# Keeping w_out's float32 blocks in DRAM and making its Winograd sums from them

## The chip, the cores and the metric

The kernel runs on one core of one Trainium2 chip. The metric is the device time of one execution in microseconds; times before and after are medians of several runs, and one further execution is recorded by the hardware profiler. The engines in the profile are PE (TensorE: matmuls) with PEld (its weight loads), DVE (VectorE), ACT (ScalarE), POOL (GpSimd) and SP (SyncE, which here only issues DMAs). An engine executes its own instructions strictly in the order written, and waits on semaphores for what other engines or DMAs deliver.

## The reference

The program is linear attention with random features, followed by a gated feed-forward layer. Cut to what matters:

```python
def phi(x):                                   # x: q or k, scaled by D ** -0.25
    h = np.einsum('bhsd,md->bhsm', x, omega) - np.sum(x * x, -1, keepdims=True) / 2
    return np.exp(h - h.max(-1, keepdims=True)) / np.sqrt(m)
q_p, k_p = phi(q_s), phi(k_s)                 # batch 8, heads 8, 576 tokens, D 64, m 128
kv = np.einsum('bhsm,bhsd->bhmd', k_p, v)
z = np.sum(k_p, axis=2)
num = np.einsum('bhsm,bhmd->bhsd', q_p, kv)
den = np.einsum('bhsm,bhm->bhs', q_p, z)[..., None] + 1e-06
x = (num / den) -> (4608 tokens, 512)
h = x @ w_in                                  # 512 x 2048, float64 in memory
g = h * np.tanh(softplus(h))
out = (g @ w_out).astype(np.float32)          # 2048 x 512, float64 in memory
```

## The kernel before

The 4608 tokens are worked in 18 chunks of 256. Matrix products are done in float16: each float32 operand is split into a high half (a cast, `cast`, L71) and a low half (the rest, `rest`, L80), and three of the four half products are summed. PE alternates between two streams: pieces of `ff_in(c)` (x times w_in, L804) and pieces of `ff_out(c-1)` (g times w_out, L1133). Between them stand the feature products of k and q (L416, with ek, eq, mxk, mxq as their results on VectorE) and the attention products (pkv L536, pn L587). Chunk 0 is computed in plain float32 (`ff_in(0)`, `ff_out0`) while the weights are still being scaled and split.

**Chunks 15, 16 and 17** use Strassen-Winograd: both products are done as seven products of half-sized blocks instead of eight (`ff_in7`, `ff_out7`). For this, sums of w_in's blocks (s1 to s4) and of w_out's blocks (t1 to t4) are needed. They are made in advance, during the chunks from 2 on, sent to DRAM as high and low float16 halves, and fetched again late in the kernel (`ask_sum`, `fetch_t`).

**How the weights come in.** A weight block is 1 MB of float64 words; there are eight blocks of w_in and eight of w_out. `w_task` (L200) loads a block, and turns it into float32 with integer operations on ScalarE (L211) and VectorE (L213, L217). The largest absolute value of each block is taken (L224 for w_in, L226 for w_out). When all eight are there, a power of two is made of the largest (`w_scale`: am_w L239, then, for w_out, over PE: row_w L136 and every_w L148), and `w_split` (L249) scales each block and splits it into its two halves. The splits write over the float32 blocks: after `w_split` the slots hold only the halves.

**How the sums are made.** `t_make(j)`, j from 0 to 3, makes the four sums for one pair of w_out's blocks, `s_make(gr, hb)` those of one pair of w_in's. Both call `sums_make` (L832). The operands are read as halves, so a difference of two blocks is two differences and an addition. Each result is cast (ScalarE) and its rest taken (VectorE) into a tile `xs`, and sent to DRAM by SP.

**What sets the order.** The program is written as generators on an agenda. A slot is one call of `step()` (L1230), 16 of them a chunk; `yield n` puts a generator to sleep for n slots. The makes are started by the loop at L1321 to L1323: first the four `t_make`, then the four `s_make`, 19 slots apart, from 40 slots after the end of chunk 0:

```python
makes = [(t_make, (j,)) for j in range(4)] + [(s_make, (i // 2, i % 2)) for i in range(4)]
for i, (fn, arg) in enumerate(makes):
    at(slot[0] + 40 + 19 * i, lambda fn=fn, arg=arg: start(fn(*arg)))
```

The framework's planner then places each engine's instructions by this order and by its own estimate of when operands are ready. Tiles with one tag share a fixed number of buffers: `ht` has five (`HB`), used by the hidden layer's tiles `h` and by the makes; `xs` has two; the PSUM tag `a` has four, shared by the feature and attention products.

Of the kernel before, what the change touches and what calls it, by code (L numbers as in the profile page):

```python
# [9 lines left out]
F16 = mybir.dt.float16  # L10
F32 = mybir.dt.float32
# [4 lines left out]
ALU = mybir.AluOpType  # L16
# [14 lines left out]
def tile_kernel(  # L31
# [10 lines left out]
    nc = tc.nc  # L42
    P = 128
    NT, D, H, _ = qT.shape
    B, HP, _, _, S = kT.shape
    M = omT.shape[1]
    DM, DF = w_in.shape
# [14 lines left out]
    sb = ctx.enter_context(tc.tile_pool(name="sb", bufs=2))  # L62
# [4 lines left out]
    dram = ctx.enter_context(tc.tile_pool(name="dram", bufs=1, space=bass.MemoryType.DRAM))  # L67

    act, dve, pool = nc.scalar, nc.vector, nc.gpsimd

    def cast(eng, out, in_, scale=1.0):  # L71

        if eng is act:
            act.activation(out, in_, AF.Copy, scale=scale)  # L74
        elif isinstance(scale, float) and scale == 1.0:
            eng.tensor_copy(out, in_)  # L76
        else:
            eng.tensor_scalar_mul(out, in_, scale)

    def rest(eng, out, in_, hi, scale=1.0):  # L80

        if isinstance(scale, float) and scale == 1.0:
            eng.tensor_tensor(out=out, in0=in_, in1=hi, op=ALU.subtract)  # L83
        else:
            eng.scalar_tensor_tensor(  # L85
                out=out, in0=in_, scalar=scale, in1=hi, op0=ALU.mult, op1=ALU.subtract
            )
# [85 lines left out]
    NB = 8  # L173
    BW = KT * DF // NB
# [3 lines left out]
    def flat32(slot):  # L178
        return slot.rearrange("p a b -> p (a b)").bitcast(F32)

    def fetch_w(n, i, dma):
        src = w_src[n](i)


        at = ({0: 0, 1: 1, 2: 2, 3: 3}, {7: 0, 6: 1, 3: 0})[n].get(i)
        if at is not None:
            raw = wo_t[:, 2 * at:2 * at + 2].rearrange("p a b c -> p (a b c)").bitcast(I64)
        else:
            raw = sb.tile([P, BW], I64, tag="g", name=f"raw{i}", bufs=GB)
        dma.dma_start(out=raw.rearrange("p (a b) -> p a b", b=src.shape[2]), in_=src)  # L190
        return raw

    @contextmanager
    def behind(nth, first=0):
        with ExitStack() as st:
            for ins in anchors.get(nth, ())[first:]:
                st.enter_context(tc.issue_after(ins))
            yield

    def w_task(i, name):  # L200

        n = 0 if name == "wi" else 1
        raw = loaded.pop(f"w{n}_{i}", None) or fetch_w(n, i, w_dma)
        yield W_LOAD
        word = raw.bitcast(I32).rearrange("p (n two) -> p n two", two=2)
        low, high = word[:, :, 0], word[:, :, 1]
        dst = flat32(slots[w_at(n, i)])
        di = dst.bitcast(I32)
        with behind(AP[i] if n == 0 else None):
            m = high.bitcast(F32)  # L210
            act.activation(m, m, AF.Prelu, scale=2.0 ** -112, alpha=-(2.0 ** 32))  # L211
        with behind((AS, AO)[n][i], 1):
            dve.tensor_single_scalar(out=di, in_=low, scalar=29, op=ALU.logical_shift_right)  # L213
        yield W_GAP
        did("w", n, i)
        with behind((AN, AO)[n][i], 1):
            dve.scalar_tensor_tensor(  # L217
                out=di, in0=high, scalar=3, in1=di, op0=ALU.logical_shift_left, op1=ALU.bitwise_or
            )
        if n == 0:  # L220
            yield WSUM[i]
            rough = sb.tile([P, BW], F16, tag="xs", name=f"rough{i}", bufs=2)
            with behind(AP[i]):
                act.activation(rough, dst, AF.Abs, accum_out=wmax[n][:, i:i + 1])  # L224
            return
        dve.tensor_reduce(  # L226
            out=wmax[n][:, i:i + 1], in_=dst, axis=AX.X, op=ALU.max, apply_absolute_value=True
        )

    def w_at(n, i):  # L230

        return i + 1 if n == 0 else NB + i
# [37 lines left out]
    def did(*key):  # L270
        done[key] = done.get(key, 0) + 1

    def must(n, *key):
        assert done.get(key, 0) >= n, key
# [24 lines left out]
    for i in range(2):  # L299
        t = const.tile([P, 2, 10, D1], F16, name=f"vb{i}")  # L300
# [526 lines left out]
    sums = {}  # L827

    def block(sl, a, row):
        return sl[:, a, row * BW // 2:(row + 1) * BW // 2]  # L830

    def sums_make(key, blocks, first, shape):  # L832
        n = BW // 2
        must(1, "s", 0, NB - 1)
        must(1, "s", 1, 0)
        t = sb.tile([P, 2, n], F32, tag="ht", name=f"s{key[0]}_{key[1]}", bufs=HB)
        s, u = (t[:, i].rearrange("p (a b) -> p a b", a=shape) for i in range(2))
        b11, b12, b21, b22 = blocks

        def tt(out, in0, in1, op=ALU.subtract):  # L840
            dve.tensor_tensor(out=out, in0=in0, in1=in1, op=op)

        def send(op, src):
            o = sb.tile([P, 2, n], F16, tag="xs", name=f"{op}_{key[0]}_{key[1]}", bufs=2)
            cast(act, o[:, 0], src)
            yield 1
            rest(dve, o[:, 1], src, o[:, 0])
            sums[key[0], key[1], op] = dram.tile([P, 2, n], F16, name=f"d{op}_{key[0]}_{key[1]}")
            nc.sync.dma_start(out=sums[key[0], key[1], op], in_=o)
            yield 1  # L850

        ops = ("s1", "s2", "s4", "s3") if first is ALU.add else ("t1", "t2", "t4", "t3")
        tt(s, b22(0) if first is ALU.add else b12(0), b21(0) if first is ALU.add else b11(0), first)
        yield 1
        tt(u, b22(1) if first is ALU.add else b12(1), b21(1) if first is ALU.add else b11(1), first)
        yield 1
        tt(s, s, u, ALU.add)
        yield from send(ops[0], t[:, 0])
        if first is ALU.add:
            tt(s, s, b11(0))  # L860
            yield 1
            tt(s, s, b11(1))
        else:
            tt(s, b22(0), s)
            yield 1
            tt(s, s, b22(1), ALU.add)
        yield from send(ops[1], t[:, 0])
        last = b12 if first is ALU.add else b21
        tt(u, last(0), s)
        yield 1  # L870
        tt(u, u, last(1), ALU.add)
        yield from send(ops[2], t[:, 1])
        pair = (b11, b21) if first is ALU.add else (b22, b12)
        tt(s, pair[0](0), pair[1](0))
        yield 1
        tt(u, pair[0](1), pair[1](1))
        yield 1
        tt(s, s, u, ALU.add)
        yield from send(ops[3], t[:, 0])
        did("sums" if first is ALU.add else "tsums")  # L880

    def s_make(gr, hb):
        sl1, sl2 = slots[4 * gr + hb], slots[4 * gr + 2 + hb]
        blocks = [
            lambda a, sl=sl, row=row: block(sl, a, row).rearrange("p (a b) -> p a b", a=2)
            for sl in (sl1, sl2) for row in range(2)
        ]
        return sums_make((gr, hb), blocks, ALU.add, 2)

    def t_make(j):  # L890
        blocks = [
            lambda a, f=f, m=m: wo_block(j, a, f, m) for f in range(2) for m in range(2)
        ]
        return sums_make(("w", j), blocks, ALU.subtract, 2)

    def wo_block(j, a, half, m):

        sl = slots[NB + 1 + 4 * half + j]
        return sl[:, a].rearrange("p (f m) -> p f m", f=2)[:, :, m * DM // 2:(m + 1) * DM // 2]
# [270 lines left out]
    GB, HB, QB = 4, 5, 1  # L1170
# [76 lines left out]
    for t in range(NT):  # L1247
        last = (t * P + P - 1) // S
# [21 lines left out]
    s_w = [None, None]  # L1270
# [8 lines left out]
    for what in PREL.split():  # L1279
        i = int(what[1:] or 0)  # L1280
# [12 lines left out]
    for i in range(NB):  # L1293
        start(w_task(i, "wi"), WIS[i])
    for i in reversed(range(1, NB)):
        start(w_task(i, "wo"), WOS[i])
# [9 lines left out]
    next(fi, None)  # L1306
    fi, fo = ff_in(1), ff_out0()
    start(w_task(0, "wo"))
    at(slot[0] + W_LOAD + W_GAP + 2, scale_w, 1)
    for j in range(8):  # L1310
# [4 lines left out]
    for j in range(8):  # L1315
# [3 lines left out]
        step()  # L1319
    next(fo, None)  # L1320
# [3 lines that stand above are left out]
# [62 lines left out]
```

## Time and profile before

| | us |
|---|---|
| median of 3 runs | 932.29 (931.63, 932.29, 934.01) |
| profiled execution | 936.42 |
| its span, first to last instruction | 934.6 |
| mean granted clock of TensorE | 0.998 of full speed |

In the profile a row of a group gives the line, the engine, the operation, output<-inputs by the program's names, shapes, the count, then the busy time in us, the mean duration of one in ns, and the engine's idle time just before them with what ended it. A row of the timeline gives the start in us from the span's start, the length in us, the engine, and in brackets the idle time before it with what released it. A timeline row can merge several instructions of one kind (x12 is twelve of them). A row of the waits gives who waited for whom, the total in us, the number of times, and the longest. A row of windows gives a stretch and the busy us of each engine in it.

### The profile page before, as it was taken

To read this page: it belongs to the slowest core of one execution; us is meant where nothing else is said; L and a number is where in the kernel's file an instruction comes from. 1 tells how busy PE (TensorE), PEld (TensorE's weight loads), DVE (VectorE), ACT (ScalarE), POOL (GpSimd) and SP (SyncE) were. 2 spreads that over 40 slices of the span, in tenths; PEclk is the share of its full clock that TensorE was granted. 3 is DMA by queue.
4 is the path that set the end of the run, shared out by engine and by line. 5 is a ranking of instruction groups with operands and counts; after the bars stand their busy time and mean duration, and the time that the engine had idled before them with its cause. 6 is when DMAs were issued, how large, how long until landed. Compare 5 with 4: busy or idle time off the path is not lost. (4 is left out here: it accounts for less than half of the span.)

```text
span 934.6 us, 21079 instructions
## 1 busy us (share of the span) xinstructions
PE 919.6 (98%) x8795; PEld 686.1 (73%) x8795; DVE 701.7 (75%) x1196; ACT 666.3 (71%) x889; POOL 216.0 (23%) x133
## 2 busy tenths in 40 slices
PE   9899999999999999899999999999999999999998
PEld 6688766677777777677777777777777777679997
DVE  4899786987769588787687757878688756668774
ACT  6988778776876967778777777788786866345442
POOL 0000123432432133222223134231241232200000
PEclk9999999999999999999999999999999999999999
DMA  9897135424532356223443254513432146972521
GB/s 308 272 280 227 50 60 120 83 86 80 111 86 84 74 112 144 65 78 89 103 116 86 77 115 104 137 49 103 106 70 91 35 116 140 237 192 92 165 63 46
DMA packets 153055, 108.69 MB, mean 116 GB/s; under 512 B 112832, under 2 KB 125248, under 8 KB 152960
## 3 DMA queue, kind: packets, MB, share of 16 engines
q1 hardware_dynamic: 152640, 106.75, 44.1%
q8 instruction: 69, 1.13, 0.5%
q10 hardware_dynamic: 320, 0.59, 0.2%
q14 instruction: 26, 0.21, 0.1%
HBM read 63.14 MB, written 17.83 MB: 87 GB/s over the span
## 5 line engine op out<-in xcount | busy, mean ns | idle before, releaser
L804 PE MATMUL ph<-xT,w 128*128 128x256 f16 (+1 forms) x2816 | 342.4, 278 | 0.9 <-ACT xT L738 0.9
L1133 PE MATMUL po<-wo,g 128*128 128x512 f16 x1344 | 310.2, 381 | 0.0
L804 PEld LDWEIGHTS <-w 128*128 128x128 f16 x2688 | 260.9, 98 | 46.6 <-issue 1.4
L1133 PEld LDWEIGHTS <-g 128*128 128x128 f16 x1344 | 127.5, 98 | 133.7 <-issue 1.6
L83 POOL TENSOR_TENSOR sq<-fq,sq 64x1024 f16<-64x1024 f32 x31 | 71.2, 2296 | 258.5 <-ACT sq L74 178.3
L991 ACT ACTIVATE h<-ph,us 128x512 f32<-128x512 f32 (+3 forms) x152 | 83.1, 573 | 49.2 <-PE ph L804 48.3
L85 DVE SCALAR_TENSOR_TENSOR g<-h,us,g 128x1024 f16<-128x1024 f32 (+3 forms) x76 | 106.3, 1408 | 13.4 <-ACT g L74 12.9
L83 POOL TENSOR_TENSOR sk<-fk,sk 64x1152 f16<-64x1152 f32 x24 | 60.0, 2498 | 88.9 <-ACT sk L74 76.8
L83 POOL TENSOR_TENSOR xs<-x,xs 128x512 f16<-128x512 f32 (+1 forms) x34 | 40.5, 1191 | 149.0 <-DVE xs L76 97.3
L991 ACT ACT_TABLE_LOAD x56 | 71.8, 1283 | 1.0
L83 DVE TENSOR_TENSOR qn<-eq,qn 128x1024 f16<-128x1024 f32 x31 | 42.9, 1384 | 36.5 <-ACT qn L74 36.5
L456 ACT ACT_TABLE_LOAD x54 | 69.3, 1283 | 1.0
L441 DVE TENSOR_REDUCE mxq<-pq 128x4 f32<-128x512 f32 x72 | 46.7, 683 | 22.3 <-PE pq L416 20.5
L941 PEld LDWEIGHTS <-w 128*128 128x128 f16 x1008 | 59.0, 98 | 2.9 <-issue 0.2
L456 ACT ACTIVATE ek<-ek,lnt 128x1152 f32<-128x1152 f32 x24 | 30.1, 1256 | 42.5 <-DVE ek L450 42.4
L74 ACT ACTIVATE g<-h,us 128x1024 f16<-128x1024 f32 (+3 forms) x64 | 58.2, 933 | 0.8
L441 DVE TENSOR_REDUCE mxk<-pk 128x4 f32<-128x512 f32 (+1 forms) x96 | 49.5, 548 | 9.2 <-PE pk L431 4.6
L456 ACT ACTIVATE eq<-eq,lnt 128x1024 f32<-128x1024 f32 x31 | 35.6, 1149 | 25.8 <-DVE eq L450 25.5
L83 POOL TENSOR_TENSOR vb<-vf,vb 128x640 f16<-128x640 f32 x24 | 38.5, 1607 | 63.3 <-DVE vb L76 53.4
L83 DVE TENSOR_TENSOR kp<-ek,kp 128x1152 f16<-128x1152 f32 x24 | 34.2, 1423 | 25.2 <-ACT kp L74 25.2
L1080 PEld LDWEIGHTS <-gb 128*128 128x128 f16 x504 | 48.3, 98 | 5.2
L991 ACT ACTIVATE h<-h,us 128x1024 f32<-128x1024 f32 (+2 forms) x16 | 14.7, 930 | 48.0 <-DVE h L951 48.0
(183 smaller groups left out, 1350.3 us busy)
## 6 DMA issues: line engine op xcount, KB each, us to landing
w<-ds SPq DMA_DIRECT2D x48, 256.0 KB, 3.5
vf<-in_vL_dram SPq DMA_DIRECT2D x32, 325.0 KB, 3.1
out_dram<-o SPq DMA_DIRECT2D x36, 256.0 KB, 2.3
fq<-in_qT_dram SPq DMA_DIRECT2D x31, 256.0 KB, 3.5
fk<-in_kT_dram SPq DMA_DIRECT2D x24, 256.0 KB, 3.7
raw<-in_w_out_dram SPq DMA_DIRECT2D x5, 1024.0 KB, 5.5
wo<-in_w_in_dram SPq DMA_DIRECT2D x4, 1024.0 KB, 10.9
raw<-in_w_in_dram SPq DMA_DIRECT2D x4, 1024.0 KB, 15.4
```

The source lines that it names most:

```text
L74: act.activation(out, in_, AF.Copy, scale=scale)
L83: eng.tensor_tensor(out=out, in0=in_, in1=hi, op=ALU.subtract)
L85: eng.scalar_tensor_tensor(out=out, in0=in_, scalar=scale, in1=hi, op0=ALU.mult, op1=ALU.subtract)
L441: sub = dve.tensor_reduce(out=mx[:, lo:hi], in_=pp[:, :m, :], axis=AX.X, op=ALU.max, negate=by_act)
L456: last = act.activation(e, e, AF.Exp, bias=lnt)
L804: last = nc.tensor.matmul(out=ph[:, i, :], lhsT=wi(a, k, f) if c else wi0(k, f), rhs=xT[c][:, y, k, :] if c else xT0()[:, k, :], start=n = ...
L941: last = nc.tensor.matmul(out=ph[:, i, :], lhsT=left(gr, op_l, i, a, k), rhs=x_region(c, r)[:, y, k0 + k, :], start=n == 0, stop=n == len( ...
L991: act.activation(h[:, :, lo:hi], ph[:, :, lo:hi], AF.Mish, scale=us[:, 0:1])
L1080: nc.tensor.matmul(out=ps, lhsT=gT[c, n][:, i, a, f, :], rhs=rhs, start=f == 0 and (a, y) == (1, 0), stop=f == FG - 1 and (a, y) == (0, 0),)
L1133: last = nc.tensor.matmul(out=po[i], lhsT=gT[c, gr][:, a, f % FG, i * P:(i + 1) * P], rhs=wo(y, f), start=f == 0 and (a, y) == parts[0], s ...
```

## The change

w_out's float32 blocks are written to DRAM by GpSimd's queue as soon as each is complete, in `w_task`. `t_make` loads the two float32 blocks that it needs from there into two `ht` tiles, waits three slots, and takes four differences, each in place and each of whole float32 blocks: t1 = b12 - b11, t3 = b22 - b12, t2 = b22 - b11 and t4 = b21 - t2. That is 4 operations per make, 16 in all, where there were 10 and 40. As these blocks are not scaled, the scale is applied in the cast and in the rest.

`s_make` still reads halves, but each sum goes on from the last (s3, then s2, s4, s1), so it takes 9 operations, 36 in all, where there were 10 and 40. It yields 13 slots in all where it yielded 14; `t_make` yields 11 where it yielded 14. When the makes start is unchanged.

```diff
         dve.tensor_reduce(
             out=wmax[n][:, i:i + 1], in_=dst, axis=AX.X, op=ALU.max, apply_absolute_value=True
         )
+        kept[i] = dram.tile([P, BW], F32, name=f"kept{i}")
+        nc.gpsimd.dma_start(out=kept[i], in_=dst)
+
+    kept = {}
...
-    def sums_make(key, blocks, first, shape):
+    def sum_send(key, op, src, scale=1.0):
         n = BW // 2
+        o = sb.tile([P, 2, n], F16, tag="xs", name=f"{op}_{key[0]}_{key[1]}", bufs=2)
+        parts = (o[:, a] for a in range(2))
+        if len(src.shape) == 3:
+            parts = (p.rearrange("p (a b) -> p a b", a=2) for p in parts)
+        high, low = parts
+        cast(act, high, src, scale)
+        yield 1
+        rest(dve, low, src, high, scale)
+        sums[key[0], key[1], op] = dram.tile([P, 2, n], F16, name=f"d{op}_{key[0]}_{key[1]}")
+        nc.sync.dma_start(out=sums[key[0], key[1], op], in_=o)
+        yield 1
+
+    def sum_tt(out, in0, in1, op=ALU.subtract):
+        dve.tensor_tensor(out=out, in0=in0, in1=in1, op=op)
+
+    def s_make(gr, hb):
         must(1, "s", 0, NB - 1)
+        sl1, sl2 = slots[4 * gr + hb], slots[4 * gr + 2 + hb]
+        b11, b12, b21, b22 = (
+            lambda a, sl=sl, row=row: block(sl, a, row) for sl in (sl1, sl2) for row in range(2)
+        )
+        t = sb.tile([P, 2, BW // 2], F32, tag="ht", name=f"s{gr}_{hb}", bufs=HB)
+        s, u = t[:, 0], t[:, 1]
+        key = (gr, hb)
+        sum_tt(s, b11(0), b21(0))
+        yield 1
+        sum_tt(u, b11(1), b21(1))
+        yield 1
+        sum_tt(s, s, u, ALU.add)
+        yield from sum_send(key, "s3", s)
+        sum_tt(s, b22(0), s)
+        yield 1
+        sum_tt(s, s, b22(1), ALU.add)
+        yield from sum_send(key, "s2", s)
+        sum_tt(u, b12(0), s)
+        yield 1
+        sum_tt(u, u, b12(1), ALU.add)
+        yield from sum_send(key, "s4", u)
+        sum_tt(s, s, b11(0), ALU.add)
+        yield 1
+        sum_tt(s, s, b11(1), ALU.add)
+        yield from sum_send(key, "s1", s)
+        did("sums")
+
+    def t_make(j):
         must(1, "s", 1, 0)
...
+        b = []
+        for half in range(2):
+            t = sb.tile([P, BW], F32, tag="ht", name=f"t{j}_{half}", bufs=HB)
+            nc.sync.dma_start(out=t, in_=kept[j + 4 * half])
+            v = t.rearrange("p (f m) -> p f m", f=2)
+            b += [v[:, :, m * DM // 2:(m + 1) * DM // 2] for m in range(2)]
+        b11, b12, b21, b22 = b
+        yield 3
+        for op, out, in0, in1 in (
+            ("t1", b11, b12, b11), ("t3", b12, b22, b12), ("t2", b22, b22, b11), ("t4", b21, b21, b22)
+        ):
+            sum_tt(out, in0, in1)
+            yield from sum_send(("w", j), op, out, s_w[1])
+        did("tsums")
```

More of the change, by code (lines that the diff above doesn't have):

```diff
@@ L830, in block @@
         return sl[:, a, row * BW // 2:(row + 1) * BW // 2]
-    def sums_make(key, blocks, first, shape):
+    def sum_send(key, op, src, scale=1.0):
         n = BW // 2
-        must(1, "s", 0, NB - 1)
-        must(1, "s", 1, 0)
[L836 to L894, printed above, removed]
+        o = sb.tile([P, 2, n], F16, tag="xs", name=f"{op}_{key[0]}_{key[1]}", bufs=2)
```

## The prediction

> **What bounds the kernel now.** The page's first part, then busy time by stretches cut where the sums are made: four for w_out's sums (266 to 508 us), one for w_in's (508 to 716). Columns: length, then busy us of PE, PEld, DVE, ACT, POOL.
>
> ```profile
> PE 919.6 (98%) x8795; PEld 686.1 (73%) x8795; DVE 701.7 (75%) x1196; ACT 666.3 (71%) x889; POOL 216.0 (23%) x133
> ...
> 266.00:326.00 60.00, 60.00 (x608) 43.80 (x606) 44.49 (x68) 47.98 (x62) 14.87 (x8) 1.00 0.28 74
> 326.00:393.00 67.00, 64.14 (x579) 44.99 (x578) 56.06 (x94) 48.08 (x58) 22.57 (x13) 0.97 0.50 108
> 393.00:460.00 67.00, 67.00 (x623) 48.08 (x622) 50.35 (x76) 50.92 (x61) 14.58 (x8) 1.00 0.37 94
> 460.00:508.00 48.00, 48.00 (x463) 35.05 (x462) 40.24 (x70) 36.34 (x40) 16.11 (x10) 1.00 0.37 92
> 508.00:716.00 208.00, 208.00 (x1957) 149.32 (x1956) 157.54 (x268) 157.49 (x187) 63.78 (x33) 1.00 0.40 98
> ```
>
> TensorE is the bound: in four of the five stretches it has no gap at all, so VectorE work taken out there is worth nothing. One stretch is different: 326 to 393 us lost 2.86 us of PE, and its granted clock is 0.97. The waits of PE name the cause, and the timeline shows it.
>
> ```profile
> PE pn L587 <- DVE ek L450: 2.7, 1, 2.7
> ```
>
> ```profile
> 368.33 2.75 PE L1133 MATMUL po<-wo,g 128*128 128x512 f16 x12
> 371.58 2.42 POOL L83 TENSOR_TENSOR sk<-fk,sk 64x1152 f16<-64x1152 f32 x1 [1.62 <-ACT sk L74]
> 371.69 2.85 DVE L841 TENSOR_TENSOR sw<-wo 128x512 f32<-128x512 f16 x1
> 373.54 0.54 PE L587 MATMUL pn<-kv,qp 128*128 128x65 f16 x12
> 374.58 0.69 DVE L841 TENSOR_TENSOR sw<-sw 128x512 f32<-128x512 f32 x1
> 375.19 0.88 DVE L441 TENSOR_REDUCE mxk<-pk 128x4 f32<-128x512 f32 x2
> 375.99 0.88 DVE L450 TENSOR_TENSOR ek<-pk,mxk 128x512 f32<-128x512 f32 x2
> 376.73 0.55 PE L587 MATMUL pn<-kv,qp 128*128 128x65 f16 x12 [2.65 <-DVE ek L450]
> 377.11 4.44 PE L1133 MATMUL po<-wo,g 128*128 128x512 f16 x12
> ```
>
> The stretch after it, in the columns of the first fence (the last three are granted clock, DMA share and GB/s):
>
> ```profile
> 376.80:380.20 3.40, 3.40 (x22) 1.56 (x23) 1.43 (x4) 1.94 (x2) 0.00 (x0) 0.68 0.01 2
> ```
>
> The second half of pn needs a PSUM buffer that ek's subtraction empties. In front of that subtraction on VectorE stand two operations of w_out's sums (L841). The first began 0.11 us after GpSimd's sk and ended 0.54 us after sk's end: 2.85 us for what otherwise takes 0.69. PE stood 2.65 us, and then ran 12 matmuls in 4.44 us, not 2.75: the granted clock fell to 0.68 in the stretch after the stall. Price of this one event: 2.65 + 1.69 = 4.34 us.
>
> The rule behind the 2.85 us is in the Trainium skill ("SBUF — State Buffer", section on the two separate sides): a VectorE operation with two SBUF inputs and a GpSimd operation that reads SBUF exclude each other for a whole instruction. The trace agrees. By that rule the new differences, which have two SBUF inputs as well, stay exposed; this is the third rival below.
>
> **The change part by part.**
>
> (1) w_out's sums on VectorE. Groups of operations, busy us and mean ns:
>
> ```profile
> L841 DVE TENSOR_TENSOR sw<-wo 128x512 f32<-128x512 f16 x16 | 20.1, 1256 | 0.1
> L841 DVE TENSOR_TENSOR s<-s,w 128x512 f32<-128x512 f32 x12 | 8.2, 688 | 0.3
> L841 DVE TENSOR_TENSOR sw<-sw,wo 128x512 f32<-128x512 f32 x8 | 6.0, 748 | 0.2
> L841 DVE TENSOR_TENSOR sw<-sw 128x512 f32<-128x512 f32 x8 | 5.5, 686 | 0.1
> L841 DVE TENSOR_TENSOR sw<-wo,sw 128x512 f32<-128x512 f16 x8 | 5.5, 682 | 0.1
> ...
> L83 DVE TENSOR_TENSOR t_w<-sw,t_w 128x512 f16<-128x512 f32 x16 | 16.6, 1035 | 1.3 <-ACT t_w L74 1.2
> L85 DVE SCALAR_TENSOR_TENSOR gb<-h,us,gb 128x512 f16<-128x512 f32 x28 | 20.4, 747 | 0.9 <-ACT gb L74 0.2
> ```
>
> Removed: 20.1 + 6.0 + 5.5 + 5.5 = 37.1 us in 40 operations. Added: 16 at 0.69 (the f32 row) = 11.0. The 16 low halves become three-operand ones: 0.75 by gb against 0.68 for an undisturbed TENSOR_TENSOR, 16 x 0.07 = +1.1. ScalarE's 16 casts stay, with a scale. VectorE saves 25.0 us. Worth on the path: only where VectorE holds PE up, so the event at 376.73.
>
> Is the event gone? The makes start 19 slots apart:
>
> ```profile
> 269.56 0.68 DVE L841 TENSOR_TENSOR sw<-wo 128x512 f32<-128x512 f16 x1
> ...
> 329.28 0.68 DVE L841 TENSOR_TENSOR sw<-wo 128x512 f32<-128x512 f16 x1
> ```
>
> 59.7 us / 19 = 3.1 us a slot here. The old make yields 14 slots, so its last sums stood at the 12th and 13th, near 370. The new one loads, yields 3, and has four differences at slots 3, 5, 7 and 9, its last low half at 10: 329.3 + 10 x 3.1 = 361, with a few us of drift 365. So nothing of it stands before mxk at 371.69, and VectorE gets there 2.85 + 0.69 us earlier (0.68 more for the low half at 370.69). 3.54 covers the 2.65 us stall. What is late next: pn's first matmul then follows its predecessor directly, and no other PE gap in the 450 us is longer than 0.2 us. Gain in the profiled execution: 4.34 us; bounds 0 (another operation falls in the same place) and 4.55 (with the 0.2 us that this stretch lost besides: 2.86 - 2.65).
>
> On the clock: the Trainium skill ("TensorE: Matmul & The Clock Gate", Part 1) wants about 3.4 us without work before the clock halves. By it the stall would be worth 2.65 us alone and the profiled sum would end 1.7 us higher. The trace disagrees: 2.65 us were enough.
>
> (2) w_in's sums: 36 operations instead of 40, four at 0.69 = 2.8 us of VectorE, in a stretch where PE has 208.00 of 208.00. Worth 0; cover gone, 2.8.
>
> (3) Eight loads of 512 KB on SP, two per make, ahead of each make. The rows that bound them, and the waits they could run into:
>
> ```profile
> dt_w<-t_w SPq DMA_DIRECT2D x16, 256.0 KB, 2.8
> raw<-in_w_out_dram SPq DMA_DIRECT2D x5, 1024.0 KB, 5.5
> ...
> SPq L357 <- POOL sq L83: 97.9, 17, 10.9
> ...
> DVE vmx L324 <- DMA vf<-in_vL_dram: 19.4, 11, 4.2
> ```
>
> Between 2.8 and 5.5 us each, 4 taken, before a first use 3 slots (9.4 us) later. Behind them on SP stand transposes and q/k/v loads, each 0.3 to 0.6 us later per issue. Each make holds two of the five h buffers where it held one, for about 7 and 9 slots; a chunk uses one per 4 slots, so three remain for some 12 slots. Worth 0.
>
> (4) Eight stores of 512 KB issued by GpSimd, as each float32 block of w_out is ready, between 60 and 101 us. No row shows a store from that queue. The stage and the narrowest place I find in it:
>
> ```profile
> 60.00:70.00 10.00, 10.00 (x62) 8.03 (x60) 9.74 (x12) 9.58 (x17) 0.00 (x0) 1.00 1.06 347
> 70.00:80.00 10.00, 10.00 (x69) 8.65 (x69) 9.27 (x15) 9.96 (x19) 0.00 (x0) 1.00 0.71 242
> 80.00:90.00 10.00, 10.00 (x80) 8.52 (x78) 10.00 (x13) 7.66 (x17) 0.27 (x1) 1.00 0.82 253
> 90.00:101.00 11.00, 11.00 (x82) 8.95 (x81) 7.86 (x14) 10.57 (x17) 1.85 (x1) 1.00 0.22 62
> ...
> 85.36 0.54 SPq L190 DMA_DIRECT2D raw<-in_w_out_dram  x1
> ...
> 98.04 1.18 ACT L211 ACTIVATE raw<-raw 128x1024 f32<-128x1024 f32 x1
> ...
> 103.99 0.15 DVE L239 TENSOR_REDUCE am_w<-wmax 128x1 f32<-128x8 f32 x1
> ...
> 106.75 0.27 PE L136 MATMUL row_w<-ident,am_w 128*1 128x128 f32 x1
> ```
>
> 8 x 128 x 4096 bytes = 4.2 MB; at 347 GB/s that is 12.1 us of full transfer. Free is 0 + 2.9 + 1.8 + 8.6 = 13.3 us, most of it after 90. So the loads of the stage are pushed back by some us. The last block of w_out is asked for at 85.36 and used at 98.04; at twice its group's 5.5 us it lands at 96.4, and after that there are 2.6 us (104.14 to 106.75) before PE needs am_w. GpSimd has only 2.1 us of work from 60 to 101, so what waits behind a store on it is little. Worth between -0 (a store frees nothing) and +4.3 (a stall with a clock drop, as at 376.73); I take 0, nearer to these covers.
>
> Sum, profiled: 936.42 - 4.34 + 0 = 932.1 us. The three runs before have 932.29 as median, 4.13 below the profiled execution, almost exactly the price of the one stall. I read this as: the event hangs on 0.11 us between two engines, fell badly in the profiled execution and not in the median run. Then the median has nothing to lose: **932.1 us, no change.** A measurement of this kernel can tell about 0.3%, 2.8 us, from no change.
>
> **The rivals.**
>
> *The stall is in the timed runs too* (and profiling itself costs the 4.13): 932.29 - 4.34 = 928.0, faster. For it: engines follow PE in fixed order, so the same 0.11 us should recur. Against: 932.1 without it fits 932.29, and 934.01 among the runs looks like one that has part of it. 0.32.
>
> *The stores crowd the first 101 us* and w_out's last block comes over 10 us late: am_w misses PE's 106.75. For it: DMA share 1.06 at 60 to 70, VectorE 29.0 of 30 us busy, no slack to catch up. Against: the covers above. Price some 2.6 us and up, with a clock drop 4.3: 934.7 to 936.4, taken as 935.6. 0.08.
>
> *The stall moves, slower*: the new make's first difference stands in VectorE's fixed order and waits for its block, which SP may issue only after a wait of up to 10.9 us (the sq row); with 4 us of transfer it is 5.5 us later than the 9.4 us allow. Or one of the 16 meets a GpSimd operation. It decides from the point where VectorE is held some 2.7 us while q's and k's PSUM buffers are all in use. Against: waits of up to 4.2 us for vf's DMA (11 of them) cost PE nothing. Price one event, 4.34: 932.1 + 4.3 = 936.4. 0.15.
>
> **How the numbers follow.** No change 0.45, with its own range 930.5 to 933.9 (the runs before spread 931.63 to 934.01, and edits (2) to (4) may take or give 1 us). The range for 8 in 10 must take in most of the first rival and half of the last: 927.6 to 936.4. Faster by over 0.3%: 0.32 and a little of the main case's edge, 0.33; slower 0.22 (0.15 + 0.08, less what of it stays under 2.8 us); within 0.45.
>
> **What would show it.** The waits of PE hold no pn or other wait over 1 us between 266 and 716 us, the clock is 1.00 throughout, and the profiled execution ends near 932 while the median stays there: right. A profiled execution at 932 with a median at 928: the first rival. VectorE's busy time should fall by 25.0 + 2.8 us to about 674. PE gaps between 60 and 110 us speak for the stores, a wait of VectorE for the kept blocks' loads with a PE wait behind it for the third rival. The forecast is wrong if the median moves by over 2.8 us.

## The result, and the profile after

The changed kernel is slower: 942.93 us (median of 6 runs, 940.01 to 945.46) against 933.33 us for the kernel before (6 runs, 931.63 to 934.01). The ratio is 1.0105, with a 95% interval of 1.0083 to 1.0126. The forecast was no change, 932.1 us; 942.93 lies above the upper end of its range, 936.4.

The profiled execution of the changed kernel took 942.98 us, with a span of 941.2 us (before: 936.42 and 934.6). First the page's part on busy time, then windows with the forecast's borders, which hold w_out's sums (266 to 508 us) and w_in's (508 to 716). Columns: length, busy us of PE, PEld, DVE, ACT and POOL, then granted clock, DMA share and GB/s.

```profile
PE 920.7 (98%) x8795; PEld 687.0 (73%) x8795; DVE 686.7 (73%) x1168; ACT 669.3 (71%) x889; POOL 226.8 (24%) x141
```

```profile
266.00:326.00 60.00, 60.00 (x579) 43.23 (x577) 40.97 (x65) 47.85 (x62) 14.49 (x8) 1.00 0.32 91
326.00:393.00 67.00, 67.00 (x657) 48.10 (x655) 53.97 (x92) 55.23 (x65) 25.27 (x14) 1.00 0.58 132
393.00:460.00 67.00, 67.00 (x623) 48.09 (x621) 42.66 (x66) 49.31 (x56) 14.90 (x8) 1.00 0.44 113
460.00:508.00 48.00, 44.03 (x399) 31.27 (x399) 39.15 (x64) 33.81 (x37) 16.29 (x8) 0.96 0.36 100
508.00:716.00 208.00, 208.00 (x1982) 149.81 (x1981) 155.46 (x265) 157.89 (x188) 65.19 (x33) 1.00 0.39 98
```

The stretch that the forecast worked on, 326 to 393 us, is now clean: 67.00 of 67.00, clock 1.00. VectorE did get 15.0 us of work less (701.7 to 686.7). But the stretch after the next lost 3.97 us of PE, and outside the forecast's borders there is a second loss. The waits of PE name both.

```profile
PE pn L591 <- DMA qp<-qn: 6.1, 4, 3.9
PE ph L808 <- ACT g L74: 2.0, 1, 2.0
```

**The early place.** Windows of 20 us, first of the kernel before, then of the changed one:

```profile
60.00:80.00 20.00, 20.00 (x128) 16.68 (x127) 19.02 (x26) 19.54 (x35) 0.00 (x0) 1.00 0.88 295
80.00:100.00 20.00, 20.00 (x153) 16.73 (x151) 17.38 (x25) 17.25 (x32) 2.12 (x1) 1.00 0.53 160
```

```profile
60.00:80.00 20.00, 20.00 (x130) 16.80 (x128) 19.27 (x26) 18.90 (x33) 2.93 (x5) 1.00 1.02 359
80.00:100.00 20.00, 18.01 (x125) 14.55 (x124) 15.66 (x22) 14.15 (x26) 3.25 (x4) 0.91 0.72 252
```

The DMA share of 60 to 80 us went from 0.88 to 1.02, and PE, which had no gap there before, lost 1.99 us in the next 20 with a clock of 0.91. The DMA part of the changed kernel's trace (KB each, median us from issue to landing) shows who pays:

```profile
raw<-in_w_out_dram SPq DMA_DIRECT2D x5, 1024.0 KB, 7.6
...
t<-kept SPq DMA_DIRECT2D x8, 512.0 KB, 4.8
...
kept<-wo POOLq DMA_DIRECT2D x7, 512.0 KB, 7.6
```

w_out's own loads take 7.6 us in the median, where the kernel before has 5.5. One of them comes too late for an engine that works strictly in order, as the changed kernel's timeline shows:

```profile
74.84 0.38 SPq L190 DMA_DIRECT2D raw<-in_w_out_dram  x1
...
83.36 1.14 ACT L211 ACTIVATE raw<-raw 128x1024 f32<-128x1024 f32 x1 [2.08 <-DMA raw<-in_w_out_dram]
...
84.40 0.58 ACT L74 ACTIVATE g<-ph 128x512 f32<-128x512 f32 x1
...
85.03 0.70 PE L808 MATMUL ph<-xT,w 128*128 128x256 f32 x2 [1.99 <-ACT g L74]
```

The two rows that answer to the first two, in the timeline of the kernel before:

```profile
75.61 0.37 SPq L190 DMA_DIRECT2D raw<-in_w_out_dram  x1
...
80.95 1.29 ACT L211 ACTIVATE raw<-raw 128x1024 f32<-128x1024 f32 x1
```

There ScalarE began the conversion without waiting. In the changed kernel the load was issued earlier, at 74.84 instead of 75.61, but it took 8.4 us to land where it had taken 5.2, and ScalarE stood 2.08 us for it. Behind it in ScalarE's queue stands the copy `g<-ph` that empties one of the two PSUM buffers of `ph`. PE needs that buffer at 85.03, and has waited 1.99 us.

That the stores share the engines of the loads is also a rule of the Trainium skill ("DMA: Bandwidth & Descriptors", section "Issuing engines are not separate DMA queues"): transfers started by GpSimd run on the same 16 DMA engines as those of SP, and interleave with them. The trace agrees: 5.5 us became 7.6.

**The late place.** VectorE's timeline in the fourth `t_make`, then GpSimd's, then those of ScalarE, SP and PE, all of the changed kernel:

```profile
461.87 0.69 DVE L851 TENSOR_TENSOR t<-t 128x512 f32<-128x512 f32 x1 [1.08 <-DMA t<-kept]
...
463.62 3.71 DVE L851 TENSOR_TENSOR t<-t,t 128x512 f32<-128x512 f32 x2
467.26 0.22 DVE L605 TENSOR_SCALAR rd<-pn 128x4 f32<-128x4 f32 x2
467.40 2.71 DVE L851 TENSOR_TENSOR t<-t 128x512 f32<-128x512 f32 x1
...
474.67 0.68 DVE L454 TENSOR_TENSOR eq<-pq,mxq 128x512 f32<-128x512 f32 x1
```

```profile
463.39 3.40 POOL L83 TENSOR_TENSOR vb<-vf,vb 128x640 f16<-128x640 f32 x2 [8.45 <-DVE vb L76]
466.87 2.69 POOL L83 TENSOR_TENSOR sk<-fk,sk 64x1152 f16<-64x1152 f32 x1
```

```profile
475.38 1.15 ACT L460 ACTIVATE eq<-eq,lnt 128x1024 f32<-128x1024 f32 x1 [6.91 <-DVE eq L454]
...
480.79 1.34 SPq L576 DMA_TRANSPOSE qp<-qn  x1
...
485.26 1.25 PE L591 MATMUL pn<-kv,qp 128*128 128x65 f16 x24 [3.90 <-DMA qp<-qn]
486.33 4.09 PE L1136 MATMUL po<-wo,g 128*128 128x512 f16 x12
```

All four differences of this make stand on VectorE within 8.24 us (461.87 to 470.11), with no low half between them. They take 0.69 + 3.71 + 2.71 = 7.11 us, where four undisturbed ones would take 4 x 0.69 = 2.76: the last three run beside GpSimd's `vb` and `sk`. What hangs on VectorE then slips in a row: ScalarE waits 6.91 us for `eq`, the transpose of `qn` is issued at 480.79, and PE's `pn` waits 3.90 us for it, with 12 matmuls in 4.09 us behind, where 2.75 is usual.

The three rows that answer to `eq`, the transpose and `pn` in the kernel before, where PE lost nothing in this place:

```profile
468.47 0.68 DVE L450 TENSOR_TENSOR eq<-pq,mxq 128x512 f32<-128x512 f32 x1
...
477.05 1.34 SPq L572 DMA_TRANSPOSE qp<-qn  x1
...
481.54 0.91 PE L587 MATMUL pn<-kv,qp 128*128 128x65 f16 x24
```

The transpose landed at 481.47, 0.07 us before `pn` began, so there was no cover behind it. In the changed kernel `eq` comes 6.20 us later and the transpose 3.74, and nearly all of the 3.74 shows in PE's wait.

### The profile page after: what moved, and what is told of

It reads as the page before. It is cut to its first block, busy times and chain, and to the rows that moved or that the text cites. A ratio compares the mean times of both kernels' runs of the same rounds, so it can differ in the third digit from the quotient of the medians.

```text
span 941.2 us, 21101 instructions
## 1 busy us (share of the span) xinstructions
PE 920.7 (98%) x8795; PEld 687.0 (73%) x8795; DVE 686.7 (73%) x1168; ACT 669.3 (71%) x889; POOL 226.8 (24%) x141
## 5 line engine op out<-in xcount | busy, mean ns | idle before, releaser
L85 DVE SCALAR_TENSOR_TENSOR g<-h,us,g 128x1024 f16<-128x1024 f32 (+3 forms) x76 | 103.4, 1371 | 15.0 <-ACT g L74 14.5
L83 POOL TENSOR_TENSOR sk<-fk,sk 64x1152 f16<-64x1152 f32 x24 | 62.0, 2581 | 89.5 <-ACT sk L74 80.5
```

Source lines behind the costliest of these rows:

```text
L85: eng.scalar_tensor_tensor(out=out, in0=in_, scalar=scale, in1=hi, op0=ALU.mult, op1=ALU.subtract)
```

## The experiments

Two theories were on record before the runs. S: the eight stores delay the early loads. T: the new differences, bunched on VectorE, make the fourth make stall PE. A third candidate was the end of the kernel: in the profiled execution the last store landed about 1.2 us later than usual. In the kernels made from the one before (`stores_only`, `stores_twice`, `stores_quarter`) the stored blocks are read by nobody, so they do extra work and leave none out. PE has the same instructions in the same order in the profiles of all ten kernels, so the PE waits compare one to one. Each ratio is to the kernel before as it ran beside that group: 933.33 us for the changed kernel, 934.45 (31 runs) for the first four kernels below, 933.43 (24 runs) for the last four.

### The stores alone, and the four kernels of a two-by-two table

`stores_only` is the kernel before with the changed kernel's stores:

```diff
             out=wmax[n][:, i:i + 1], in_=dst, axis=AX.X, op=ALU.max, apply_absolute_value=True
         )
+        kept[i] = dram.tile([P, BW], F32, name=f"kept{i}")
+        nc.gpsimd.dma_start(out=kept[i], in_=dst)
+
+    kept = {}
```

> The kernel before with the eight stores of w_out's float32 blocks added, which nothing reads; everything else, and the order on every engine but GpSimd, as before. Theory S (the stores crowd the DMA queues at 60 to 95 us, a block of w_out lands late, ScalarE waits for it in order, TensorE stalls at about 85 us and its clock halves): 933.3 + 1.99 + 1.7 + 1.1 = about 938, with a wait of PE ph on ACT g and a granted clock under 1 between 80 and 100 us. Theory T (the whole loss lies in the new differences of w_out's sums, bunched on VectorE and blocked there by GpSimd): 933.3, no such wait. A third, that the stores' queue lengthens the end of the program: about +1.2 us between the last matmul and the end.

Measured: 937.94 us, ratio 1.0034 (1.0010 to 1.0059). The stores alone cost about a third of the loss. The waits of PE in its profile have the same row as the changed kernel's, shorter, and the loads take 7.5 us:

```profile
PE ph L808 <- ACT g L74: 1.1, 1, 1.1
```

That execution was the quickest of the ten (934.22 us), and from 80 to 100 us its clock was 1.00: the fall of the clock that theory S named isn't in it.

`stores_late` is the changed kernel with its stores behind GpSimd's part of q5, from about 92 us on instead of 60, when the last of w_out's loads has landed (at 90.98 in its profile):

```diff
         kept[i] = dram.tile([P, BW], F32, name=f"kept{i}")
-        nc.gpsimd.dma_start(out=kept[i], in_=dst)
+        while "q5" not in pool_ins:
+            yield 1
+        with tc.issue_after(pool_ins["q5"]):
+            nc.gpsimd.dma_start(out=kept[i], in_=dst)
```

> The changed kernel with its eight stores queued behind GpSimd's rest of q5 (about 92 us), when the DMA engines have fallen to a share of 0.22 or less. Theory S: the stall at 85 us and its clock drop are gone, 942.9 - 4.8 = about 938. Theory T: 942.9, as the differences are unchanged and the stall at 485 us stays.

Measured: 940.3 us, ratio 1.0058 (1.0029 to 1.0088), between what S (938) and T (942.9) expected, so both have a part. The wait at 85 us is gone: 20.00 of 20.00 us in both windows, and the loads are back at 5.7 us. The bunched differences and the late stall are all there: of VectorE's timeline and PE's,

```profile
459.22 3.71 DVE L855 TENSOR_TENSOR t<-t,t 128x512 f32<-128x512 f32 x2
463.00 2.71 DVE L855 TENSOR_TENSOR t<-t 128x512 f32<-128x512 f32 x1
```

```profile
480.79 1.50 PE L595 MATMUL pn<-kv,qp 128*128 128x65 f16 x24 [3.83 <-DMA qp<-qn]
```

`t_paced` is the changed kernel with each difference tied behind the low half of the sum before it on VectorE; the stores stay:

```diff
+            with ExitStack() as st:
+                if op != "t1":
+                    st.enter_context(tc.issue_after(low_made[0]))
-            sum_tt(out, in0, in1)
+                sum_tt(out, in0, in1)
```

> The changed kernel with each difference of w_out's sums queued on VectorE behind the low half of the sum before it, so that the four of a make no longer stand back to back; stores as changed. Theory T: the stall at 485 us (3.9 us and a clock drop of 1.3 to 1.7) is gone, about 937.5. Theory S: 942.9, the stall at 85 us stays.

Measured: 936.2 us, ratio 1.0005 (0.9982 to 1.0028), near the 937.5 of theory T. Here the stall at 485 us is gone and the early one is left (PE `ph` waits 1.54 us at 85.58). The differences still meet GpSimd now and then, but one at a time, and PE doesn't notice:

```profile
475.66 0.68 DVE L853 TENSOR_TENSOR t<-t,t 128x512 f32<-128x512 f32 x1
481.71 2.85 DVE L853 TENSOR_TENSOR t<-t,t 128x512 f32<-128x512 f32 x1
486.95 0.68 DVE L853 TENSOR_TENSOR t<-t 128x512 f32<-128x512 f32 x1
```

`late_paced` has both edits.

> Both at once: stores behind q5's rest and the differences spaced. If S and T together are the loss: 933 or a little under, 932 to 934. If the loss lies in neither (the loads of the kept blocks on SP, the scale in cast and rest, w_in's sums): 938 or more.

Measured: 933.38 us, ratio 0.9984 (0.9952 to 1.0016). Its profile has a span of 931.7 us, a clock of 1.00 and after the first 60 us no wait of PE longer than 1.30 us:

```profile
60.00:80.00 20.00, 20.00 (x131) 16.61 (x129) 19.02 (x25) 19.49 (x33) 0.00 (x0) 1.00 0.88 297
80.00:100.00 20.00, 20.00 (x152) 16.80 (x151) 17.35 (x25) 17.16 (x33) 6.21 (x8) 1.00 0.77 265
```

What follows. In a table of ratios:

| | stores as changed | stores late |
|---|---|---|
| differences as changed | 1.0105 | 1.0058 |
| differences spaced | 1.0005 | 0.9984 |

Down a column is T: 0.0100 and 0.0074, 7 to 9 us, the larger part. Along a row is S: 0.0047 and 0.0021, with 0.0034 for the stores alone: 2 to 4 us. The first ratio was taken against 933.33 us and the other three against 934.45; straight between the medians T is 6.7 and 6.9 us, and S 2.6 and 2.8. With both taken away nothing of the loss is left, so the two account for it, within the intervals. The intervals of the changed kernel and `t_paced` don't touch, nor do those of the changed kernel and `stores_only`; those of the changed kernel and `stores_late` do, barely (1.0083 against 1.0088). The third candidate falls: from PE's last matmul to the end of the span, the changed kernel's profiled execution took 4.84 us, and the four others here, which all have the stores, 3.65 to 4.12.

Part of T is clock. Span times mean granted clock is an estimate of the span at full clock, as PE is busy nearly all the time (good to half a us, since the clock is given to 0.001). Its medians are 936.3 us for the changed kernel, 934.6 for `stores_late`, 931.8 for `t_paced` and 930.4 for `late_paced`. By this estimate T without its clock loss is 4.5 and 4.2 us, close to the one stall of 3.9.

`late_paced`, with all of the change's savings on VectorE and neither of the two stalls, has the time of the kernel before. So the saved VectorE work itself is worth nothing that can be measured, and no version here beats the kernel before by more than can be told.

### w_in's half alone

`s_only` is the kernel before with the new `sum_send`, `sum_tt` and `s_make`; `t_make` is the old one and there are no stores.

```diff
+    def s_make(gr, hb):
...
+        sum_tt(s, b11(0), b21(0))
...
-        return sums_make((gr, hb), blocks, ALU.add, 2)
```

> The kernel before with w_in's new sums alone (36 operations), w_out's sums and no stores of the changed kernel. Both theories put the whole loss into w_out's half (S: the eight stores beside the early loads, about 3 us; T: the differences bunched in the fourth make, 7 to 9 us), so both expect the time of the kernel before, 0.997 to 1.003 of it. If w_in's part carries a loss of its own, the time is above 1.003.

Measured: 933.38 us, ratio 0.9996 (0.9974 to 1.0018). As expected: w_in's half neither costs nor gives.

### The fourth make alone

`paced_last` spaces the differences in the fourth make only:

```diff
-                if op != "t1":
+                if op != "t1" and j == 3:
```

> The changed kernel with its stores as they are, and w_out's differences spaced only in the fourth make (j of 3), not in the other three. If T is the stall of the fourth make alone (PE waiting 3.90 us at 485 and the half clock behind it), this comes out as t_paced did, 1.000 of the kernel before, within 0.003. If the bunching of differences in every make costs, it lies between t_paced and the changed kernel, 1.004 to 1.010.

Measured: 936.31 us, ratio 1.0029 (1.0011 to 1.0048). It is just inside the bound that was set for "the fourth make alone", and its interval overlaps that of `t_paced`, but it also has the larger value. The medians themselves are 936.31 and 936.20 us; the ratios differ because the kernel before took 933.43 us beside one and 934.45 beside the other. So most of T (0.0076 of 0.0100 by the ratios) is the fourth make's stall, and nothing shows that the other three makes cost anything. Its profile has no PE wait over 1 us between 266 and 716 us.

### Is it the bytes or the issues?

`stores_twice` writes each block twice, `stores_quarter` a quarter of each block, both in the kernel before and with nothing read. `stores_quarter` has as many issues as `stores_only`.

```diff
+        kept[i + 8] = dram.tile([P, BW], F32, name=f"kept{i}b")
+        nc.gpsimd.dma_start(out=kept[i + 8], in_=dst)
```

```diff
-        nc.gpsimd.dma_start(out=kept[i], in_=dst)
+        nc.gpsimd.dma_start(out=kept[i][:, 0:BW // 4], in_=dst[:, 0:BW // 4])
```

> The kernel before with each of the eight blocks stored twice (8.4 MB in place of 4.2), none of it read. If S is the bytes that the stores take from the loads, the loss is at least twice that of stores_only (1.0034): 1.007 or more. If it is a fixed price of having the issues on GpSimd, about that of stores_only, 1.001 to 1.006.

> The kernel before with a quarter of each block stored (1 MB in all), none of it read; as many issues as in stores_only. If S is the bytes, about a quarter of the loss is left: 1.000 to 1.001. If it is a fixed price of the issues, about that of stores_only, 1.0034.

Measured: `stores_twice` 945.93 us (4 runs), ratio 1.0119 (1.0067 to 1.0170); `stores_quarter` 935.09 us, ratio 1.0003 (0.9981 to 1.0025). Eight issues with a quarter of the bytes cost nothing that can be measured, eight with all of them 0.34%, sixteen with twice the bytes 1.19%. The times alone don't decide, as the intervals of the first two overlap (up to 1.0025, from 1.0010) and `stores_twice` doubles the issues too. The traces say that it is the bytes. The groups of w_out's loads, of `stores_quarter` first, then of `stores_twice`, beside 5.5 us for no stores and 7.5 for `stores_only`:

```profile
raw<-in_w_out_dram SPq DMA_DIRECT2D x5, 1024.0 KB, 5.6
```

```profile
raw<-in_w_out_dram SPq DMA_DIRECT2D x5, 1024.0 KB, 10.3
```

In `stores_quarter` the block of the early place landed at 80.03, 0.33 us before ScalarE's turn, and PE doesn't wait there. In `stores_twice` the wait is longer:

```profile
87.26 1.17 ACT L211 ACTIVATE raw<-raw 128x1024 f32<-128x1024 f32 x1 [3.33 <-DMA raw<-in_w_out_dram]
...
88.96 1.13 PE L810 MATMUL ph<-xT,w 128*128 128x256 f32 x2 [3.28 <-ACT g L74]
```

PE waits 3.28 us here, and 1.1 to 2.15 in the four profiles with the early stores once. The time grows by more than that, and by the estimate above the excess is clock. Span times clock has a median of 935.5 us in `stores_twice` and 930.3 in the kernel before beside it: 5.2 us more, of 12.5 in all. Its four executions lost 1.9, 8.5, 7.5 and 12.3 us to the clock, those of the kernel before 2.6 in the mean. Why it loses so much isn't shown: the profiled execution is the one that lost 1.9.

## Why the prediction was wrong

**Right: what bounds the kernel, and that VectorE's work is worth nothing by itself.** `late_paced` keeps the savings and has the time of the kernel before (0.9984, 0.9952 to 1.0016).

**Right: the stall at 376.73 was in the profiled execution and not in the median.** It is gone in the changed kernel. But it is gone as well in the profiles of `s_only` and `stores_only`, which keep the old `t_make`, and it is back in that of `stores_quarter`:

```profile
379.93 0.84 PE L591 MATMUL pn<-kv,qp 128*128 128x65 f16 x12 [2.65 <-DVE ek L454]
380.58 4.13 PE L1137 MATMUL po<-wo,g 128*128 128x512 f16 x12
```

So the same wait, to the 2.65 us, comes in some executions and not in others, as the forecast read from 0.11 us between two engines. The first rival (928.0 us) falls: the profiled execution of `s_only`, which is without the stall, took 933.15 us, near its median of 933.38. There was nothing to win.

**Wrong, step (1): "four differences at slots 3, 5, 7 and 9".** The slots are where the program emits them. The planner moves what doesn't depend on what is between. t2 reads the tile b11, in which t1 stands by then (it is b22 - t1, and so not what the list in "The change" seems to say), and t4 reads t2; but no difference needs a low half, so nothing held t3, t2 and t4 back, and all four ran as one block. That is so in all four makes. Eight of the 16 differences, 2, 1, 2 and 3 of the makes in turn, ran beside a GpSimd operation and took 1.49 to 2.71 us; only those of the fourth make reached PE.

The forecast had this as its third rival ("one of the 16 meets a GpSimd operation"), with one event and 4.34 us, and a chance of 0.15. Its blocking was right. Its path was not: it had PE stopped by full PSUM buffers, and here PE waited for the transpose of `qn`. T is worth 7 to 9 us by the ratios. In the profiled execution the stall and the half clock behind it are 3.90 + 1.71 = 5.61 us (1.71 is half of the 3.41 us that the clock was halved).

The sum of VectorE's time shows the same step. These are the groups of the changed kernel:

```profile
L85 DVE SCALAR_TENSOR_TENSOR t_w<-t,s_w,t_w 128x512 f16<-128x512 f32 x16 | 17.9, 1129 | 0.9 <-ACT t_w L74 0.9
L851 DVE TENSOR_TENSOR t<-t 128x512 f32<-128x512 f32 x8 | 12.2, 1523 | 1.6 <-DMA t<-kept 1.5
...
L851 DVE TENSOR_TENSOR t<-t,t 128x512 f32<-128x512 f32 x8 | 7.8, 976 | 0.2
```

The low halves came out as forecast (16.6 + 1.1 = 17.7; measured 17.9). The 16 differences took 12.2 + 7.8 = 20.0 us instead of 11.0. An undisturbed duration was taken for operations of which the forecast itself said that they "stay exposed" to GpSimd. That is 9.0 of the 12.7 us by which VectorE's time missed 674.

**Right: (2) and (3).** `s_only` is 0.9996. The kept blocks' loads landed in 4.8 us in the median (4 taken), and VectorE waited for them 1.5 us in two places; PE doesn't wait for these, and `late_paced`, which has these loads, loses nothing.

**Wrong, step (4): the stores "Worth ... 0".** The bounds, 0 to +4.3, held what was measured (0.34%, 3.2 us); the value taken in them was the wrong end. The working looked for the narrowest place and named the last block and am_w. That place did hold: in the changed kernel the last block was used 3 us later (ScalarE at 101.07 instead of 98.04), am_w was done at 107.17, and PE has no gap from 99 to 108 and reaches the matmul that needs it at 109.77. The place that gave was the block before it: not the data were needed by PE, but a PSUM buffer that ScalarE would empty after it had converted that block. In the kernel before, that block landed at 80.77, 0.18 us before ScalarE's turn at 80.95, so there was no cover at all, and the group's median of 5.5 us didn't show it. The second rival ("the stores crowd the first 101 us") described the mechanism; 0.08 was too little.

**The sum.** Between the profiled executions of the changed kernel and of `late_paced`, which has neither loss, lie 941.2 - 931.7 = 9.5 us. The two stalls with their halved clocks (1.99 + 1.71 and 3.90 + 1.71) are 9.3 and the late end is 1.2; that is 1.0 too much, and what makes it up isn't settled.

**Not settled.** Whether the bunching alone, without GpSimd's operations beside it, would have stalled PE was not tried: spacing the differences takes away both at once. In the profile the blocked time is 7.11 - 2.76 = 4.35 us, more than PE's 3.90, which speaks for the blocking but doesn't show it. So does an estimate: `eq` came 6.20 us late and the transpose 3.74, so 2.46 us were covered between them; without the 4.35 blocked us `eq` would have been 1.85 us late, less than that.

## What to carry to other kernels

An instruction written between two yields is placed by what it depends on; if its position must hold, tie it to the instruction that it is to follow, and ask this of every chain that a change shortens. When a change adds transfers to a crowded stage, don't look only at who needs the delayed data last: list each transfer that lands just before its use (by 0.18 us in the early place, by 0.07 in the late one), and see what stands behind that use in the same engine's queue. Operations that stay exposed to another engine are to be costed at the mean that such operations show (1.25 us here, half of them disturbed), not at the clean duration (0.69).

## What the runs showed of the hardware

**The price of a stall depends on where it falls.** The forecast priced a stall with a fixed clock loss behind it. The traces show spells of half clock of 3.41 us, or twice that, and they begin on a grid: in the changed kernel, windows at exactly the two spells,

```profile
86.26:89.67 3.41, 3.41 (x9) 2.70 (x9) 3.41 (x4) 1.44 (x5) 0.53 (x1) 0.50 0.87 285
...
485.62:489.03 3.41, 3.41 (x26) 1.75 (x23) 3.31 (x7) 3.38 (x4) 1.39 (x1) 0.50 0.05 13
```

Between the two starts lie 399.36 us, which is 117 times 3.413. Laid over all ten profiles, the grid reads like this. Eight steps of it ran at half clock behind a step in which PE had stood idle; that idle time was 1.54 us at the least. Between 60 and 900 us no step with 1.23 us of idle or less was followed by one at half clock, but for the two spells below, ahead of which there was none at all. Nearer the start, around 35 us, steps with 1.53 us of idle had full clock behind them. In `paced_last` a longer stall than that of the changed kernel fell across a border of the grid, 1.22 us on one side and 0.92 on the other, and cost no clock:

```profile
86.66 0.70 PE L808 MATMUL ph<-xT,w 128*128 128x256 f32 x2 [2.15 <-ACT g L74]
...
87.65 4.05 PE L808 MATMUL ph<-xT,w 128*128 128x256 f32 x21
```

The same 21 matmuls took 5.74 us in the changed kernel behind its 1.99 us. That a border decides is argued from these two and the grid; no run moved a stall on purpose. The Trainium skill ("TensorE: Matmul & The Clock Gate", Part 1) has a free-running window of 3413 ns, and the grid agrees with that to 0.01 us; its threshold of about a whole idle window doesn't agree, since 1.54 us of idle were enough in `t_paced`.

**Spells without a stall.** In `t_paced` from 104.22 to 111.05 us, and in `stores_quarter` near 100 us, the clock was halved for 6.83 us while PE had work without a gap. The window of `t_paced`:

```profile
104.22:111.05 6.83, 6.83 (x22) 3.90 (x23) 4.98 (x11) 5.88 (x13) 0.74 (x1) 0.50 0.55 165
```

What sets these off is open. They are part of why executions of one kernel differ by some us: of 31 executions of the kernel before in the first group of runs, the eight with a mean clock of 1.000 lie within 932.22 to 933.88 us, and all 31 within 932.06 to 944.04.
